# Laying out the tiles of triangular blocks and their transposed inverses with the block index innermost, in a fused recurrence and feed-forward kernel

## The chip, the cores and the metric

The kernel runs on one core of one Trainium2 chip. The metric is the device time of one execution in microseconds; three executions of the kernel before gave 995.05 us as their median (995.01 to 995.82). The engines are TensorE (PE in the rows, its weight loads PEld), VectorE (DVE), ScalarE (ACT), GpSimd (POOL) and SyncE (SP), which issues most of the DMAs. They run at the same time, each through its own list of instructions in a fixed order, and wait for one another by semaphores.

## What is computed

Four batches, 768 time steps and 320 channels (8 heads of 40) go through three parts, each of which takes the one before as its input:

```python
for t in range(S):                       # 1: a gated recurrence, per head a 40x40 state
    y[:, :, t] = einsum('bhd,bhde->bhe', r_t, state)
    Sa = einsum('bhde,bhe->bhd', state, a_t)
    state = state * w_t - einsum('bhd,bhe->bhde', Sa, b_t) + einsum('bhd,bhe->bhde', v_t, k_t)
h = maximum(x @ w_in, 0)                 # 2: feed-forward, 320 to 1024 to 320
x = (h * sigmoid(conv3(h))) @ w_out      #    gated by a convolution over time
u = x + real(fft(fft(x, axis=1), axis=2))            # 3: a Fourier mixing
out = u + maximum(layernorm(u) @ w_ch1, 0) @ w_ch2   #    and a second feed-forward
```

## The kernel before, in words

The change lies in part 1, in class `Attn`. The recurrence is worked in chunks of 64 time steps: 12 chunks, 4 batches and 8 heads. Within a chunk the update can be written as a triangular system of size 64 for each head and batch, so each (chunk, batch, head) has a unit triangular matrix whose inverse is needed. A 64x64 matrix is cut into two 32x32 triangular blocks on the diagonal and one full 32x32 block beside them.

Blocks are collected in groups. `group(c)` puts chunks 0 and 1 into groups 0 and 1 by themselves and then two chunks into each of groups 2 to 6, so there are seven groups. Tiles of a group are [128, 32, 32] or [128, 32, 64] in fp32: the 128 partitions hold the two blocks of two heads (two sets of rows of 64, each with a first and a second half of 32), and the free dimension holds a block index u (16 used in groups 0 and 1, 32 in the others; u counts chunk of the group, batch and pair of heads) and a column.

- `gram` (L189) makes the products of one chunk and batch on TensorE (L203). ScalarE copies the two triangular blocks with a minus sign into the tile `l0` (L218, L220) and the full block into `l1` (L219). In chunk 0 VectorE writes `l0` (L215) and applies the mask at once. Each such instruction writes 4 blocks: 32 partitions x 128 elements. In the trace l0 and l1 are both shown as `l`.
- `grp_start` (L244) makes `l0`; for groups 0 and 1 GpSimd clears its unused half (L248).
- `inverse` (L292) turns the group: VectorE transposes every 32x32 block of `l0` into the tile `A`, in which the block index is innermost (L297); a chain of multiplications and additions on VectorE solves all blocks together (L317 and L320 for groups 2 to 6, L259 and L262 for groups 0 and 1). Then VectorE transposes `A` back: once into `t1`, block after block (L327, or L270), and twice into the two column halves of `tt`, the tile with the transposed inverses (L330; for groups 0 and 1 `inverse16` fills it with L269 and, after two rounds of small matmuls L278, with two L288 of half the size). GpSimd clears a quarter of each half of `tt` (L333). In the trace t1 is shown as `t`.
- The merge (from L334): for each half `hf` of the blocks, 32 small matmuls on TensorE (L344, into PSUM tile `bp`), two copies by ScalarE back into `t1` (L348), 32 small matmuls that read `t1` and a column half of `tt` (L357, into `mp`), and two copies by ScalarE into `tt` (L361). Groups 0 and 1 have one half, the others two.
- `stage_u` (L381) then uses `tt` in each of the 48 steps (chunk, batch): for each of four pairs of heads a weight load of 64 columns of `tt` and a matmul with 80 columns (L388). An fp32 matmul is shown in the trace as two pairs of load and matmul, so a step has 8.

The steps go on one after the other: `step` (L470) lists the stages of a step: u (L388), s (L409, then VectorE L414 and L418 and GpSimd), y (L442, L445), ut (L397), h (L372, L375), g (L428, then VectorE L432 makes `gt`, which L445 of the next step reads) and o (L456, L460, then VectorE L463). `run` (L542) spreads the gram of a later chunk, the chain of the next inverse and a stream of weight preparation for parts 2 and 3 (`prep`, L684 to L741) between the stages. Both the order in which `run` issues and a planner that works with its own estimates of durations set the order of instructions on each engine before the program starts; on the chip it is fixed. Parts 2 and 3 (`Moe`) begin when the last step's output is stored.

Of the kernel before, what the change touches and what calls it, by code (L numbers as in the profile page):

```python
# [18 lines left out]
B, H, S, D = 4, 8, 768, 40  # L19
C = 64  # L20
NCH = S // C
NG = 3
HG = 3
P3 = HG * D
# [56 lines left out]
class Attn:  # L81
    def __init__(self, ctx, tc, ins, xd):
        self.tc, self.nc, self.xd = tc, tc.nc, xd
        self.i = ins
        nc = self.nc
# [25 lines left out]
        self.slots = {}  # L111
        for k, n, m, shape in (("x", 10, 4, [128, 2, NG * P3]), ("lk", 8, 4, [128, 2, 4, C]), ("tt", 2, 1, [128, 32, 64])):
            self.slots[k] = [mid[j >= m].tile(shape, F32, name=f"{k}{j}") for j in range(n)]
# [75 lines left out]
    def gram(self, c, b):  # L189
        nc = self.nc  # L190
# [6 lines left out]
        gidx, j = group(c)  # L197
# [8 lines left out]
        gv = gp.rearrange("p (q e t) -> p q e t", q=4, e=2)  # L206
        l0, l1 = g["l0"], g["l1"]
        for p in range(2):
# [35 lines left out]
    def grp_start(self, gidx):  # L244
        l0 = self.early.tile([128, 32, 32], F32, name="l0", tag="l0", bufs=1)
        l1 = self.early.tile([128, 32, 32], F32, name="l1", tag="l1", bufs=2)
        if gidx < 2:
            self.nc.gpsimd.memset(l0[:, 16:32], 0.0)  # L248
        self.grp[gidx] = dict(l0=l0, l1=l1)
# [15 lines left out]
    def inverse16(self, fl, t1, tt):  # L265
        nc = self.nc
        A = fl[:, 0:1024].rearrange("p (t s) -> p t s", s=32)
        at = tt[:, :, 32:64]
        nc.vector.transpose(at.rearrange("p u t -> p t u"), A)  # L269
        self.last = nc.vector.transpose(t1.rearrange("p u j -> p j u"), A.rearrange("p t j -> p j t"))  # L270
        yield
        m1 = self.early.tile([128, 16, 16], F32, name="m1", tag="tmp", bufs=2)
        for k in range(2):
            xp = self.pst("xd")
            for u in range(16):
                for q in range(4):
                    r = slice(32 * q, 32 * q + (32 if k else 16))
                    nc.tensor.matmul(xp[32 * q:32 * q + 32, 16 * u:16 * u + 16], at[r, u],  # L278
                                     m1[r, u] if k else t1[r, u, 0:16], start=True, stop=True)
# [7 lines left out]
        for i in (1, 0):  # L287
            nc.vector.transpose(tt[:, 0:16, 32 * i:32 * i + 32], t1[:, 0:16])  # L288
            yield


    def inverse(self, gidx):  # L292
# [3 lines left out]
        A = fl[:, 0:1024].rearrange("p (t s) -> p t s", s=32)  # L296
        self.first = nc.vector.transpose(A, g["l0"].rearrange("p u t -> p t u"))  # L297
        yield
# [14 lines left out]
        else:  # L313
# [15 lines left out]
            for i in (1, 0):  # L329
                nc.vector.transpose(tt[:, :, 32 * i:32 * i + 32].rearrange("p u t -> p t u"), A)  # L330
                yield
        for p in range(2):
            nc.gpsimd.memset(tt[64 * p + 32:64 * p + 64, :, 0:32], 0.0)  # L333
        yield "merge"  # L334
# [15 lines left out]
        for hf in range(nhf):  # L350
            xp = self.pst("mp")
            for u in range(16):
                for p in range(2):
                    r0 = slice(64 * p, 64 * p + 32)
                    r1 = slice(64 * p + 32, 64 * p + 64)
                    uu = hf * 16 + u
                    nc.tensor.matmul(xp[r0, 32 * u:32 * u + 32], bm[r1, uu], tt[r1, uu, 32:64],  # L357
                                     start=True, stop=True)
            for p in range(2):
                r0 = slice(64 * p, 64 * p + 32)  # L360
                nc.scalar.copy(tt[r0, hf * 16:hf * 16 + 16, 32:64],  # L361
                               xp[r0].rearrange("p (u t) -> p u t", t=32))
            yield
# [17 lines left out]
    def stage_u(self, c, b):  # L381
# [5 lines left out]
        for q in range(4):  # L387
            nc.tensor.matmul(hu[64:128, 80 * q:80 * q + 80], tt[:, (j * B + b) * 4 + q],  # L388
                             self.hbd[b][:, q].rearrange("p a b -> p (a b)"), start=True, stop=True)
# [973 lines left out]
```

## Time and profile before

| | |
|---|---|
| median of three executions | 995.05 us |
| the profiled execution: time | 997.03 us |
| its span, first to last instruction | 995.3 us |
| PE busy (weight loads apart) | 906.7 us, 91% |
| PEld busy | 818.7 us, 82% |
| DVE busy | 684.1 us, 69% |
| ACT busy | 520.7 us, 52% |
| POOL busy | 456.5 us, 46% |
[...]

Matmuls overlap in a pipeline, so "PE busy" is the time in which some matmul was under way and not a measure of its work. [...] A time of an instruction is its own duration; where a row of the timeline joins several (x4, x128), its time is from the first one's start to the last one's end. "[1.05 <-DVE gt L432]" means that the engine was idle for 1.05 us before the instruction, and that by the semaphores it was VectorE's L432 on `gt` that ended the wait. Part 1 takes the first 497 us, parts 2 and 3 the rest.

### The profile page before, as it was taken

To read this page: it belongs to the slowest core of one execution; us is meant where nothing else is said; L and a number is where in the kernel's file an instruction comes from. 1 tells how busy PE (TensorE), PEld (TensorE's weight loads), DVE (VectorE), ACT (ScalarE), POOL (GpSimd) and SP (SyncE) were. 2 spreads that over 40 slices of the span, in tenths; PEclk is the share of its full clock that TensorE was granted. 3 is DMA by queue.
4 is the path that set the end of the run, shared out by engine and by line. 5 is a ranking of instruction groups with operands and counts; after the bars stand their busy time and mean duration, and the time that the engine had idled before them with its cause. 6 is when DMAs were issued, how large, how long until landed. Compare 5 with 4: busy or idle time off the path is not lost. (4 is left out here: it accounts for less than half of the span.)

```text
span 995.3 us, 21859 instructions
## 1 busy us (share of the span) xinstructions
PE 906.7 (91%) x8178; PEld 818.7 (82%) x8178; DVE 684.1 (69%) x1322; ACT 520.7 (52%) x1448; POOL 456.5 (46%) x528
## 2 busy tenths in 40 slices
PE   5568698999989999999999699989999999999997
PEld 3557587888878888998888587777879999999997
DVE  8895997997996996881278697879684535424321
ACT  5668387676766577334376566567464431212211
POOL 6575375665665464343168566765562121101000
PEclk8667599997997999999999899998999999999999
DMA  9624346565555364339344643112105000000000
GB/s 224 178 77 128 90 126 178 154 161 147 150 138 152 98 169 114 87 98 255 81 126 134 187 141 114 54 50 70 41 1 172 20 1 21 20 20 21 20 14 31
DMA packets 102878, 101.15 MB, mean 102 GB/s; under 512 B 47160, under 2 KB 89003, under 8 KB 102763
## 3 DMA queue, kind: packets, MB, share of 16 engines
q1 hardware_dynamic: 100795, 94.73, 34.3%
q0 software_dynamic: 1968, 4.93, 1.6%
q8 instruction: 67, 1.10, 0.5%
q14 instruction: 48, 0.39, 0.2%
HBM read 74.81 MB, written 20.76 MB: 96 GB/s over the span
## 5 line engine op out<-in xcount | busy, mean ns | idle before, releaser
L831 DVE SCALAR_TENSOR_TENSOR c<-h,cw,c 128x384 f32<-128x384 f32 x128 | 113.3, 890 | 21.0 <-ACT c L829 17.4
L1085 DVE SCALAR_TENSOR_TENSOR gl<-hp,gh 128x384 fp32r<-128x384 f32 x80 | 44.4, 557 | 111.3 <-ACT gh L1084 111.2
L848 PE MATMUL acc<-w_out_f,z 128*128 128x320 f32 x384 | 118.0, 446 | 2.8 <-POOL z L837 1.1
L1084 ACT ACTIVATE gh<-hp 128x384 fp32r<-128x384 f32 x80 | 39.3, 492 | 149.8 <-PE hp L655 149.6
L848 PEld LDWEIGHTS acc<-w_out_f,z 128*128 128x128 f32 x384 | 73.5, 196 | 27.0 <-ACT x L853 1.8
L655 PE MATMUL hp<-xh,w_in_h 128*128 128x386 f32 x192 | 76.3, 397 | 14.3 <-ACT h L822 14.3
L655 PE MATMUL hp<-uh,w_ch_h 128*128 128x384 f32 x240 | 82.3, 343 | 0.0
L655 PE MATMUL hp<-ul,w_ch_h 128*128 128x384 f32 x240 | 81.0, 337 | 0.0
L1108 POOL DMA_INDIRECT out<-o,rows x12 | 11.7, 978 | 150.8 <-DVE o L1103 131.9
L317 DVE TENSOR_TENSOR tmp<-A 128x30 f32<-128x30 f32 (+9 forms) x150 | 77.1, 514 | 3.3
L320 DVE TENSOR_TENSOR A<-A,tmp 128x30 f32<-128x30 f32 (+9 forms) x150 | 76.8, 512 | 3.5
L203 PE MATMUL gram<-abd,kb 120*128 120x192 f32 (+1 forms) x288 | 64.6, 371 | 13.4 <-DMA w<-in_w 6.9
L419 POOL TENSOR_TENSOR st<-st,sm 120x360 f32<-120x360 f32 x40 | 48.3, 1208 | 56.9 <-DVE sm L418 53.0
L1098 PE MATMUL acc<-w_ch_h,gh 128*128 128x320 f32 x240 | 73.2, 312 | 0.0
L1098 PE MATMUL acc<-w_ch_l,gh 128*128 128x320 f32 x240 | 73.0, 309 | 0.0
L203 PEld LDWEIGHTS gram<-abd,kb 120*128 120x128 f32 x288 | 56.0, 227 | 17.3 <-POOL lk L223 9.7
L655 PE MATMUL hp<-xl,w_in_h 128*128 128x386 f32 x192 | 67.1, 349 | 0.0
L736 POOL TENSOR_TENSOR pm<-pm,py 128x160 int32<-128x160 int32 (+2 forms) x64 | 45.0, 703 | 44.0 <-DVE pm L734 17.1
L832 ACT ACTIVATE c<-c 128x384 f32<-128x384 f32 x64 | 33.4, 522 | 60.5 <-DVE c L831 60.3
L161 POOL TENSOR_TENSOR kb<-kb,vx 120x768 f32<-120x768 f32 x24 | 44.0, 1833 | 45.5 <-DMA kb<-in_kb 25.3
L445 PE MATMUL yp<-x,gt 128*64 128x40 f32 x768 | 54.8, 233 | 10.1 <-DVE gt L432 10.1
L445 PEld LDWEIGHTS yp<-x,gt 128*64 128x64 f32 x768 | 51.0, 143 | 13.2 <-DVE gt L432 11.9
(226 smaller groups left out, 2585.9 us busy)
## 6 DMA issues: line engine op xcount, KB each, us to landing
kb<-in_kb SPq DMA_DIRECT2D x24, 360.0 KB
vbd<-in_vbd SPq DMA_DIRECT2D x24, 320.0 KB
xd<-xo SPq DMA_DIRECT2D x56, 90.0 KB
w<-in_w SPq DMA_DIRECT2D x24, 185.6 KB
a<-in_a SPq DMA_DIRECT2D x24, 180.0 KB
z<-in_zv SPq DMA_DIRECT2D x24, 180.0 KB
zt<-in_vt SPq DMA_DIRECT2D x24, 180.0 KB
rbd<-in_r SPq DMA_DIRECT2D x72, 60.0 KB
```

Of the source, the lines that this page charges most:

```text
L161: self.markp = nc.gpsimd.tensor_tensor(kb, kb, vx[:, :, 2:66].unsqueeze(2).to_broadcast([P3, 6, 2, C]), op=ALU.mult)
L203: nc.tensor.matmul(gp[:, 192 * gi:192 * gi + 64 * nh], d["kb"][:, bl * NG + gi].rearrange("p a b -> p (a b)"), abd[:, 0:nh, bl * NG + gi], ...
L317: nc.vector.tensor_tensor(tmp, A[:, s + 1:32, s:s + 1].to_broadcast([128, n, s]), A[:, s:s + 1, 0:s].to_broadcast([128, n, s]), op=ALU.mult)
L320: nc.vector.tensor_tensor(A[:, s + 1:32, 0:s], A[:, s + 1:32, 0:s], tmp, op=ALU.add)
L419: nc.gpsimd.tensor_tensor(self.st[b], self.st[b], t, op=ALU.add)
L445: nc.tensor.matmul(yp[0:64, D * h:D * h + D], gt[:, h], d["x"][:, bl, D * h:D * h + D], start=(c == 0), stop=True, skip_group_check=True)
L655: nc.tensor.matmul(out, l, r, start=(j == 0), stop=(j == len(ops) - 1))
L736: nc.gpsimd.tensor_tensor(m, m, y, op=ALU.add)
L831: nc.vector.scalar_tensor_tensor(c, h[:, j:HS + j], cw[:, f, j:j + 1], c, op0=ALU.mult, op1=ALU.add)
L848: nc.tensor.matmul(self.acc[t][:, 0:DM], z[:, ts], w[:, f], start=(f == 0), stop=(f == NF1 - 1))
L1085: nc.vector.scalar_tensor_tensor(gl, hp[:, 0:HS], 0.0, gh.bitcast(F32), op0=ALU.max, op1=ALU.subtract)
L1098: nc.tensor.matmul(self.acc[t][:, 0:DM], l[:, ts], r, start=(f == 0 and j == 0), stop=(f == NF2 - 1 and j == 2))
```

## The change

The last two dimensions of `l0` and `tt` change places: `l0[partition, block, column]` becomes `l0[partition, column, block]`, `tt` likewise ([128, 32, 64] becomes [128, 64, 32]). `A`, `t1` and `l1` stay as they were. The same instructions read and write the same elements; the step from one element to the next changes:

- VectorE's L297 reads `l0`, and L330 and L269 write `tt`, in one contiguous run of 1024 where the step was 32 or 64 elements (L330, L269: 64; L297: 32). L288 (512 elements) wrote runs of 32 and now writes with a step of 32 elements.
- ScalarE's L218 and L220 and VectorE's L215 wrote `l0` in runs of 32 and now write with a step of 32 elements, so does ScalarE's L361 into `tt`.
- TensorE read contiguous columns of `tt` in L278 (weights, 32 columns), L357 (the moving operand, 32 columns) and L388 (weights, 64 columns), and now reads them with a step of 32 elements (128 bytes).
- GpSimd's L333 clears contiguous runs of 1024 in place of 32 runs of 32, and L248 clears 32 runs of 16 in place of one of 512.

```diff
@@ -109,7 +109,7 @@
         self.sm = [self.pre.tile([P3, NG, P3], F32, name=f"sm{j}") for j in range(2)]
 
         self.slots = {}
-        for k, n, m, shape in (("x", 10, 4, [128, 2, NG * P3]), ("lk", 8, 4, [128, 2, 4, C]), ("tt", 2, 1, [128, 32, 64])):
+        for k, n, m, shape in (("x", 10, 4, [128, 2, NG * P3]), ("lk", 8, 4, [128, 2, 4, C]), ("tt", 2, 1, [128, 64, 32])):
             self.slots[k] = [mid[j >= m].tile(shape, F32, name=f"{k}{j}") for j in range(n)]
         self.hf, self.late, self.markd = {}, None, None
         self.grp = {}
@@ -204,7 +204,7 @@
                              d["kb"][:, bl * NG + gi].rearrange("p a b -> p (a b)"),
                              abd[:, 0:nh, bl * NG + gi], start=True, stop=True)
         gv = gp.rearrange("p (q e t) -> p q e t", q=4, e=2)
-        l0, l1 = g["l0"], g["l1"]
+        l0, l1 = g["l0"].rearrange("p t u -> p u t"), g["l1"]
         for p in range(2):
             mul = nc.scalar.mul
             r0, r1 = slice(64 * p, 64 * p + 32), slice(64 * p + 32, 64 * p + 64)
@@ -245,7 +245,7 @@
         l0 = self.early.tile([128, 32, 32], F32, name="l0", tag="l0", bufs=1)
         l1 = self.early.tile([128, 32, 32], F32, name="l1", tag="l1", bufs=2)
         if gidx < 2:
-            self.nc.gpsimd.memset(l0[:, 16:32], 0.0)
+            self.nc.gpsimd.memset(l0[:, :, 16:32], 0.0)
         self.grp[gidx] = dict(l0=l0, l1=l1)
 
 
@@ -265,8 +265,8 @@
     def inverse16(self, fl, t1, tt):
         nc = self.nc
         A = fl[:, 0:1024].rearrange("p (t s) -> p t s", s=32)
-        at = tt[:, :, 32:64]
-        nc.vector.transpose(at.rearrange("p u t -> p t u"), A)
+        at = tt[:, 32:64]
+        nc.vector.transpose(at, A)
         self.last = nc.vector.transpose(t1.rearrange("p u j -> p j u"), A.rearrange("p t j -> p j t"))
         yield
         m1 = self.early.tile([128, 16, 16], F32, name="m1", tag="tmp", bufs=2)
@@ -275,7 +275,7 @@
             for u in range(16):
                 for q in range(4):
                     r = slice(32 * q, 32 * q + (32 if k else 16))
-                    nc.tensor.matmul(xp[32 * q:32 * q + 32, 16 * u:16 * u + 16], at[r, u],
+                    nc.tensor.matmul(xp[32 * q:32 * q + 32, 16 * u:16 * u + 16], at[r, :, u],
                                      m1[r, u] if k else t1[r, u, 0:16], start=True, stop=True)
             xv = xp[:, 0:256].rearrange("p (u s) -> p u s", s=16)
             if k == 0:
@@ -285,7 +285,7 @@
                                                op0=ALU.mult, op1=ALU.add)
             yield
         for i in (1, 0):
-            nc.vector.transpose(tt[:, 0:16, 32 * i:32 * i + 32], t1[:, 0:16])
+            nc.vector.transpose(tt[:, 32 * i:32 * i + 32, 0:16].rearrange("p t u -> p u t"), t1[:, 0:16])
             yield
 
 
@@ -294,7 +294,7 @@
         g = self.grp[gidx]
         fl = self.early.tile([128, 33 * 32], F32, name="A", tag="A", bufs=1)
         A = fl[:, 0:1024].rearrange("p (t s) -> p t s", s=32)
-        self.first = nc.vector.transpose(A, g["l0"].rearrange("p u t -> p t u"))
+        self.first = nc.vector.transpose(A, g["l0"])
         yield
 
         def new():
@@ -327,10 +327,10 @@
             nc.vector.transpose(t1.rearrange("p u j -> p j u"), A.rearrange("p t j -> p j t"))
             yield
             for i in (1, 0):
-                nc.vector.transpose(tt[:, :, 32 * i:32 * i + 32].rearrange("p u t -> p t u"), A)
+                nc.vector.transpose(tt[:, 32 * i:32 * i + 32], A)
                 yield
         for p in range(2):
-            nc.gpsimd.memset(tt[64 * p + 32:64 * p + 64, :, 0:32], 0.0)
+            nc.gpsimd.memset(tt[64 * p + 32:64 * p + 64, 0:32], 0.0)
         yield "merge"
         bm = t1
         nhf = 1 if gidx < 2 else 2
@@ -354,11 +354,11 @@
                     r0 = slice(64 * p, 64 * p + 32)
                     r1 = slice(64 * p + 32, 64 * p + 64)
                     uu = hf * 16 + u
-                    nc.tensor.matmul(xp[r0, 32 * u:32 * u + 32], bm[r1, uu], tt[r1, uu, 32:64],
+                    nc.tensor.matmul(xp[r0, 32 * u:32 * u + 32], bm[r1, uu], tt[r1, 32:64, uu],
                                      start=True, stop=True)
             for p in range(2):
                 r0 = slice(64 * p, 64 * p + 32)
-                nc.scalar.copy(tt[r0, hf * 16:hf * 16 + 16, 32:64],
+                nc.scalar.copy(tt[r0, 32:64, hf * 16:hf * 16 + 16].rearrange("p t u -> p u t"),
                                xp[r0].rearrange("p (u t) -> p u t", t=32))
             yield
 
@@ -385,7 +385,7 @@
         tt = self.grp[gidx]["tt"]
         hu = self.pst("u")
         for q in range(4):
-            nc.tensor.matmul(hu[64:128, 80 * q:80 * q + 80], tt[:, (j * B + b) * 4 + q],
+            nc.tensor.matmul(hu[64:128, 80 * q:80 * q + 80], tt[:, :, (j * B + b) * 4 + q],
                              self.hbd[b][:, q].rearrange("p a b -> p (a b)"), start=True, stop=True)
         self.mark = nc.scalar.mul(d["z"][64:128, bl, 0:DM], hu[64:128, 0:DM], -1.0)
 
```

## Rows read from the trace of the kernel before

**Rows 1.** Windows: us, busy us of PE, PEld, DVE, ACT, POOL (instructions), clock, DMA share, GB/s.
```profile
250.00:300.00 50.00, 46.34 (x423) 41.20 (x422) 48.94 (x101) 34.01 (x115) 31.07 (x36) 0.97 0.54 146
450.00:500.00 50.00, 49.44 (x518) 44.47 (x517) 11.38 (x29) 19.84 (x52) 12.50 (x17) 1.00 0.63 169
```
**Rows 2.** Timeline: start us, us, instruction. TensorE's last of part 1, first of part 2.
```profile
497.49 0.19 PE L522 MATMUL rp<-ro,rs 120*1 120x1 f32 x2
497.61 0.44 PE L655 MATMUL hp<-xh,w_in_h 128*128 128x386 f32 x1
```
**Rows 3.** Groups by form, VectorE: out<-in shapes xcount | busy us, mean ns | idle before.
```profile
L330 DVE STREAM_TRANSPOSE tt<-A 128x1024 f32<-128x1024 f32 x10 | 18.5, 1929 | 0.0
L297 DVE STREAM_TRANSPOSE A<-l 128x1024 f32<-128x1024 f32 x7 | 13.7, 1964 | 15.8 <-ACT l L220 15.8
...
L215 DVE SCALAR_TENSOR_TENSOR l<-gram,mlt 32x128 f32<-32x128 f32 x16 | 4.7, 291 | 0.4
...
L288 DVE STREAM_TRANSPOSE tt<-t 128x512 f32<-128x512 f32 x4 | 2.5, 672 | 0.0
```
**Rows 4.** Timeline: transposes and merge of group 4, partly at the lower clock.
```profile
307.63 3.71 DVE L330 STREAM_TRANSPOSE tt<-A 128x1024 f32<-128x1024 f32 x2
...
311.43 0.67 DVE L432 TENSOR_TENSOR gt<-gp,mlt 128x512 f32<-128x512 f32 x1
...
312.24 1.44 PE L428 MATMUL gp<-rbd,zt 120*128 120x192 f32 x6 [1.23 <-ACT t L348]
...
313.61 3.62 PE L357 MATMUL mp<-tt,t 32*32 32x32 f32 x128
...
315.57 1.16 ACT L361 COPY tt<-mp 32x512 f32<-32x512 f32 x2 [2.83 <-PE mp L357]
317.16 1.06 PE L388 MATMUL u<-hbd,tt 128*64 128x80 f32 x6
```
**Rows 5.** Timeline: the same in group 3.
```profile
234.12 1.82 PE L428 MATMUL gp<-rbd,zt 120*128 120x192 f32 x6 [1.05 <-DVE gt L432]
...
238.75 1.16 ACT L361 COPY tt<-mp 32x512 f32<-32x512 f32 x2
...
240.01 1.30 PE L388 MATMUL u<-hbd,tt 128*64 128x80 f32 x8
```
**Rows 6.** Timeline: a transpose of group 1 and what stood behind it.
```profile
74.57 1.90 DVE L269 STREAM_TRANSPOSE tt<-A 128x1024 f32<-128x1024 f32 x1
...
78.75 0.55 PE L409 MATMUL sp<-z,x 128*120 128x120 f32 x1 [3.40 <-DVE st L414]
```
**Rows 7.** Waits: who waited for whom, us in total, times, longest us.
```profile
DVE A L297 <- ACT l L220: 15.8, 4, 6.2
...
ACT t L348 <- DVE tt L288: 10.7, 1, 10.7
```
**Rows 8.** Timeline: the first stage u, of group 0.
```profile
60.84 1.33 PE L388 MATMUL u<-hbd,tt 128*64 128x80 f32 x8 [2.31 <-POOL tt L333]
```
**Rows 9.** By line and tile: ns min/median/max, first and last start us, form.
```profile
L220 ACT ACTIVATE l<-gram x88: 270/272/275, 28.9 to 395.3; 32x128 f32<-32x128 f32 x88
...
L278 PEld LDWEIGHTS xd<-t,tt x256: 101/115/154, 40.2 to 99.6; 16*32 16x32 f32 x128
...
L361 ACT COPY tt<-mp x24: 570/576/577, 58.6 to 449.3; 32x512 f32<-32x512 f32 x24
```
**Rows 10.** Timeline: a stage u at full clock, its eight loads and eight matmuls.
```profile
429.87 0.61 PEld L388 LDWEIGHTS u<-hbd,tt 128*64 128x64 f32 x8
429.87 0.77 PE L388 MATMUL u<-hbd,tt 128*64 128x80 f32 x8
```
**Rows 11.** Timeline: end of the merge of group 5, at full clock.
```profile
389.41 2.21 PE L357 MATMUL mp<-tt,t 32*32 32x32 f32 x128
...
390.66 2.35 ACT L361 COPY tt<-mp 32x512 f32<-32x512 f32 x4 [1.42 <-PE mp L357]
...
391.87 0.49 PE L388 MATMUL u<-hbd,tt 128*64 128x80 f32 x4 [0.25 <-ACT tt L361]
```

## The prediction, made before the change was timed

> **What bounds the kernel now.** I read the windows first, then the groups of VectorE by form, then the timeline around the places where the changed tiles are made and used. In 250 to 300 us VectorE is busy for 48.94 of 50 us and PE for 46.34; in 450 to 500 us PE is busy for 49.44 and VectorE for 11.38 [rows 1]. So part 1 is held by VectorE in some steps and by TensorE in others, and in the merges, where a group's inverses are finished, by a chain that runs through PE and ScalarE. TensorE's last matmul of part 1 starts at 497.49, the first of part 2 at 497.61 [rows 2]: parts 2 and 3 follow at once, and no changed instruction stands in them. A microsecond won or lost at the end of part 1 is counted as one at the end of the kernel.
>
> **VectorE's transposes.** The change takes the long step out of 19 transposes of 1024 elements: ten L330, seven L297 and two L269. They take 1.93 to 1.96 us each [rows 3]. No transpose of before with two contiguous sides has 1024 elements; L288, which has runs of 32 on one side, takes 0.672 us for 512 [rows 3]. Twice that is 1.34, the upper bound for 1024 contiguous elements. From L215's 128 elements in 0.291 to L288's 512 in 0.672 the slope is 0.99 ns an element and some 0.16 us are fixed; 512 more at this slope give 1.18, the lower bound. I take 1.2, as the two L288 halves of the first bound count the fixed part twice: 0.73 saved each (0.6 to 0.78), 13.9 us of VectorE's time in all. The four L288 now write with a step, as L330 does: between half of 1.93 and half of 1.93 + 0.16, 0.97 to 1.05, so 0.35 more each. L327 and L270 stay as they were.
>
> What of it lies on the path:
> 1. Group 4's two L330 end at 311.34, and L432 (`gt`), which they held up, runs 311.43 to 312.10; TensorE's L428 then starts at 312.24 after 1.23 us of idleness [rows 4]. The row names ScalarE's L348, but VectorE's end lies 0.14 us before the start. With the transposes 1.46 shorter the gap goes: 1.2 us. In group 3 the same L428 waits 1.05 us for `gt` by the row's own words [rows 5]: 1.05. In group 2 VectorE is full too, but the next wait is on ScalarE: half, 0.7. In groups 5 and 6 TensorE has other work: 0.
> 2. In group 1, TensorE's L409 is idle for 3.40 us until VectorE's L414, which stands behind L269 (and L270) in its queue [rows 6]: 0.72.
> 3. L297 starts a group's chain, and in four groups VectorE sat idle before it, 15.8 us in all, for ScalarE's L220 [rows 7]. For groups 3 to 5, whose chains end in steps that VectorE fills, I count half of 3 x 0.76: 1.1. Group 6 runs in PE's stretch: 0.
> 4. Group 0 starts the kernel: L297 and L269 win 1.48, eight L215 directly ahead of L297 write with a step and lose (128 elements x 0.71 ns, the price worked out below) 0.73. The first stage u waits for GpSimd's L333 in the end [rows 8], so of the 0.75 left I count half: 0.4.
>
> That is 5.2 us of the 13.9; the rest is covered by TensorE and by waits. Against it, group 1's L348 waits for both L288 [rows 7]: 0.7 lost.
>
> **ScalarE's writes.** L361 (512 elements, 0.576 us) and L218 and L220 (128 elements, 0.272, 176 of them) now write with a step of 128 bytes [rows 9]. No ScalarE instruction of before does that. Lower bound: nothing. Upper: what the step costs VectorE, 0.73 us / 1024 = 0.71 ns an element. VectorE's is the only stepped fp32 write in the trace, so I take it: L361 becomes 0.94, L218 and L220 0.36.
>
> **TensorE's reads.** Stage u loads 64 columns of `tt` eight times in 0.61 us and goes through in 0.77 [rows 10]: 76 ns a load, 96 ns a pair. L357 streams 32 columns 128 times in 2.21 us [rows 11], 17 ns each, two of them side by side on different rows: 35 ns for one. No load or matmul of before reads with a step. Lower bound: nothing, if the array takes a column too slowly to notice. Upper: again 0.71 ns a column, 45 ns on a load and 23 on an L357. I take the upper end, since the only stepped accesses that the trace shows all pay, whether they read (L297) or write (L330). Then a load takes 121 ns, more than the 96 of its pair, and stage u grows by 8 x 25 = 0.2 us. L357 grows from 17 to 29 ns, 0.75 us for a half group. At the lower clock it already takes 3.62 us for 128, 28 ns each [rows 4], and stage u 1.30 [rows 5], 163 ns a pair: there the step hides, and I count 0. L278's weights are 512 loads of 32 columns in groups 0 and 1 (256 shown [rows 9]), four side by side: at most 512 x 23 / 4 ns = 2.9 us. I count 0, since PE is not the late engine in that stretch (VectorE and GpSimd are [rows 6, 8]), and keep 2.9 for the range.
>
> [...]
>
> **What that does on the path.** In the merge, stage u starts right behind the first half's two L361: in group 3 copies from 238.75 to 239.91, u at 240.01 [rows 5]; in group 5 copies from 390.66, two of four done at 391.82, u at 391.87 [rows 11]. Groups 1, 2 and 6 look the same. Two copies more dear by 0.36 each delay u by 0.73 in groups 1, 2 and 3; in group 4 there are 0.4 us of slack (316.73 to 317.16 [rows 4]), so 0.4; in groups 5 and 6, where the clock is full, L357's first half adds 0.75 to it, 1.5 each. Group 0 is covered by GpSimd [rows 8]. Sum 5.5 us.
>
> Stage u at full clock: 16 steps in PE's stretch at the end and about 10 more between, where PE is busy from one u to the next. 26 x 0.2 = 5.2 us; the other 22 are hidden behind VectorE or the lower clock.
>
> The four L218 and L220 of a chunk and batch take 0.36 us more. ScalarE has room (34.0 of 50 us [rows 1]), except where L297 waits for the last of them [rows 7]: half of 3 x 0.36, 0.5. GpSimd's L333 and L248 clear as many elements as before: 0, and GpSimd is not ahead of anyone but in group 0.
>
> **The sum.** Won 5.2; lost 0.7 + 5.5 + 5.2 + 0.5 = 11.9; 6.7 us slower. The profiled execution took 997.03 us (span 995.3), so 1003.7 for it; the median of the runs is 995.05, and set on it I predict 1001.7.
>
> **Rivals.**
> - *The step is free for ScalarE and TensorE.* Then only VectorE's terms stand: 5.2 won, 0.7 lost, 4.5 faster, 990.5. [...] The point from which it decides: if L388's loads and L361 stay at 76 ns and 0.576 us. [...] Chance 0.26.
> - *Only ScalarE pays.* L361 costs 0.73 in groups 1, 2, 3, 5 and 6 and 0.4 in group 4, 4.0; with 0.5 and 0.7 it balances the 5.2: 995.1. Chance 0.17.
> - *The costs land everywhere.* Stage u pays in all 48 steps (4.4 more) and the second halves' copies, which stand before `z` on ScalarE, delay it by 0.73 in five groups (3.6): 1009.7. The same would come if u had now to wait for both halves, whose columns lie in between each other: 1.16 us of copies in five groups, 5.8 more. Chance 0.08.
> - *The transposes don't get faster*, because 32x32 blocks and not steps set their time: 5.2 lost from the sum, 1006.9. L288's 1.31 ns an element against L330's 1.88 speaks against it. Chance 0.03.
>
> **How the numbers follow.** My forecast, every price at VectorE's, has 0.46, with a range of its own of 997 to 1007: 26 steps could be 16 or 36 (2 us each way) and the halves that I counted none or whole (3). As cases of both signs hold much of the chance, the range reaches down to the free case and up to most of the dear one: 989 to 1009, which leaves out about a tenth at each end. A measurement tells about 0.2%, 2 us, from nothing. Faster: nearly all of the first rival, a fifth of the second and a little of the forecast, 0.30. Same: most of the second, a twelfth of the others, 0.17. Slower: 0.53.
>
> **What would show it.** Right, step by step: L330, L269 and L297 at 1.15 to 1.34 us, L288 near 1.0; L361 near 0.94 and L218 and L220 near 0.36; the eight loads of a stage u at full clock near 0.97 us and an L357 half near 1.85. L428's wait for `gt` in groups 3 and 4 gone, the start of u in groups 5 and 6 about 1.5 us further behind the start of L357, and TensorE's first matmul of part 2 at about 504. Wrong: if L388 and L361 keep their durations the forecast falls and the first rival stands; if the planner, which sees other tiles, puts instructions in another order, terms 1 and 3 may come out otherwise.

## The result, and the profile after

The changed kernel takes 1013.5 us (median of six runs, 1011.3 to 1018.0) against 996.8 for the kernel before: a ratio of 1.0148, with a 95% interval of 1.0116 to 1.0181. A second set of runs gave 1.0160 (1.0121 to 1.0200). That is 15 us slower, where 6.7 were forecast. The profiled execution took 1011.6 us with a span of 1009.9; before it was 997.03 and 995.3.

Both kernels issue the same instructions; only the steps between elements of the changed operands differ. VectorE, ScalarE and GpSimd show them in the same order in both traces, and TensorE too, but for some places where matmuls of stage u start among those of a neighbouring stage. First the windows of the changed kernel, with the columns of [rows 1], and the end of part 1, as [rows 2] shows it of before:

```profile
250.00:300.00 50.00, 47.65 (x424) 42.73 (x422) 48.96 (x100) 36.00 (x115) 32.20 (x35) 0.97 0.52 144
450.00:500.00 50.00, 49.65 (x537) 45.21 (x530) 8.62 (x22) 20.00 (x46) 13.26 (x20) 0.83 0.53 154
```
```profile
513.77 0.19 PE L522 MATMUL rp<-ro,rs 120*1 120x1 f32 x2
513.89 0.45 PE L655 MATMUL hp<-xh,w_in_h 128*128 128x386 f32 x1
```

Part 2 starts 16.3 us later (513.89 against 497.61), so the whole loss, and 1.7 us more, lies in part 1. In the late window TensorE is as busy as before, but its granted clock is 0.83 instead of 1.00.

The changed groups by form (columns as in [rows 3]; ScalarE's before are in [rows 9]):

```profile
L361 ACT COPY tt<-mp 32x512 f32<-32x512 f32 x24 | 24.4, 1017 | 9.9 <-PE mp L357 9.6
...
L330 DVE STREAM_TRANSPOSE tt<-A 128x1024 f32<-128x1024 f32 x10 | 11.7, 1217 | 0.0
L297 DVE STREAM_TRANSPOSE A<-l 128x1024 f32<-128x1024 f32 x7 | 8.7, 1237 | 21.1 <-ACT l L220 21.1
L215 DVE SCALAR_TENSOR_TENSOR l<-gram,mlt 32x128 f32<-32x128 f32 x16 | 6.1, 382 | 0.4
L288 DVE STREAM_TRANSPOSE tt<-t 128x512 f32<-128x512 f32 x4 | 3.8, 1018 | 0.0
```

VectorE's transposes are as fast as was hoped, 1.22 and 1.24 us where they took 1.93 and 1.96, and ScalarE's L361 is 0.44 us dearer. Note how L297's idle time grew from 15.8 to 21.1 us: part of what VectorE saved came back as waiting. Stage u in the last steps, first its weight loads, then the matmuls (timeline; [rows 10] before):

```profile
428.15 0.96 PEld L388 LDWEIGHTS u<-hbd,tt 128*64 128x64 f32 x8
```
```profile
428.16 1.11 PE L388 MATMUL u<-hbd,tt 128*64 128x80 f32 x8
```

It takes 1.11 us where it took 0.77. (Steps are counted here by stage u, 0 to 47, from one to the next; the first steps of groups 2 to 6 are 8, 16, 24, 32 and 40.) The timeline of group 4's merge ([rows 4] before) and group 5's ([rows 11]):

```profile
308.20 2.32 DVE L330 STREAM_TRANSPOSE tt<-A 128x1024 f32<-128x1024 f32 x2
...
310.65 0.67 DVE L432 TENSOR_TENSOR gt<-gp,mlt 128x512 f32<-128x512 f32 x1
...
311.89 1.08 PE L428 MATMUL gp<-rbd,zt 120*128 120x192 f32 x6
...
389.69 3.80 PE L357 MATMUL mp<-tt,t 32*32 32x32 f32 x128
...
391.71 4.08 ACT L361 COPY tt<-mp 32x512 f32<-32x512 f32 x4 [2.21 <-PE mp L357]
...
393.79 1.26 PE L388 MATMUL u<-hbd,tt 128*64 128x80 f32 x8 [0.30 <-ACT tt L361]
```

In group 4 the idle time of 1.23 us before L428 is gone, as forecast. In group 5, L357 takes 3.80 us instead of 2.21, though the clock is full (1.00 in both), and stage u starts 4.10 us behind its start instead of 2.46. Last, the step that follows each of the merges of groups 2 to 6, from one stage u to the next (windows, columns as in [rows 1]: the last three are granted clock, DMA share and GB/s):

```profile
162.40:170.25 7.85, 7.85 (x64) 6.98 (x64) 3.17 (x9) 7.27 (x19) 1.47 (x3) 0.80 0.51 147
240.85:248.89 8.04, 8.04 (x68) 7.36 (x68) 2.91 (x8) 7.22 (x19) 2.35 (x5) 0.80 0.54 142
317.06:325.60 8.54, 8.54 (x62) 7.63 (x63) 3.12 (x9) 6.36 (x17) 1.00 (x2) 0.68 0.45 123
393.79:401.74 7.95, 7.95 (x64) 7.09 (x65) 2.45 (x6) 6.56 (x17) 0.73 (x1) 0.79 0.01 2
456.08:463.69 7.61, 7.61 (x53) 6.80 (x53) 0.00 (x0) 3.92 (x8) 0.00 (x0) 0.50 0.92 275
```

The same five steps of the kernel before:

```profile
161.72:169.71 7.99, 7.99 (x64) 7.05 (x64) 4.11 (x10) 6.22 (x19) 1.58 (x3) 0.79 0.59 175
240.01:248.69 8.68, 8.68 (x69) 7.85 (x68) 4.00 (x9) 6.33 (x19) 3.40 (x5) 0.74 0.56 149
317.16:325.94 8.78, 8.78 (x67) 7.87 (x63) 3.69 (x8) 5.46 (x17) 1.32 (x2) 0.66 0.42 120
391.87:398.53 6.66, 6.38 (x64) 5.65 (x65) 2.74 (x5) 5.52 (x17) 0.73 (x1) 1.00 0.17 44
448.80:453.05 4.25, 4.25 (x54) 3.82 (x54) 0.00 (x0) 2.68 (x8) 0.00 (x0) 1.00 0.87 240
```

Before, the clock was low behind the merges of groups 2 to 4 and full behind the last two; here it falls behind all five. Together the five steps are only 3.6 us longer than before (39.99 against 36.36). Most of the loss shows in the last 16 steps, from stage u of step 32 to part 2: the kernel before, the changed kernel, its step 41 alone (the second step behind group 6's merge; 6.31 us before), and the last 16 steps in a second profile of it, which comes further below:

```profile
391.87:497.61 105.74, 104.61 (x1305) 94.44 (x1306) 55.45 (x123) 42.70 (x115) 29.98 (x41) 1.00 0.47 125
393.79:513.89 120.10, 119.19 (x1305) 108.26 (x1305) 53.60 (x123) 46.02 (x116) 29.96 (x41) 0.91 0.39 109
463.69:474.06 10.37, 10.37 (x66) 9.46 (x65) 1.43 (x4) 2.02 (x7) 1.87 (x5) 0.56 0.87 282
397.68:512.52 114.84, 113.93 (x1306) 103.75 (x1306) 53.59 (x123) 45.57 (x115) 29.98 (x41) 0.97 0.41 113
```

The stretch is 14.4 and 9.1 us longer than before; up to its start 1.9 and 5.8 us were lost.

### The profile page after: what moved, and what is told of

Its sections match the earlier page's. It is cut to its first block, busy times and chain, and to the rows that moved or that the text cites. A ratio compares the mean times of both kernels' runs of the same rounds, so it can differ in the third digit from the quotient of the medians.

```text
span 1009.9 us, 21859 instructions
## 1 busy us (share of the span) xinstructions
PE 926.2 (92%) x8178; PEld 838.3 (83%) x8178; DVE 677.0 (67%) x1322; ACT 545.3 (54%) x1448; POOL 455.9 (45%) x528
## 5 line engine op out<-in xcount | busy, mean ns | idle before, releaser
L831 DVE SCALAR_TENSOR_TENSOR c<-h,cw,c 128x384 f32<-128x384 f32 x128 | 110.3, 866 | 19.3 <-ACT c L829 15.7
L848 PE MATMUL acc<-w_out_f,z 128*128 128x320 f32 x384 | 114.2, 435 | 3.4 <-POOL z L837 1.2
L848 PEld LDWEIGHTS acc<-w_out_f,z 128*128 128x128 f32 x384 | 71.2, 190 | 26.4 <-POOL z L835 2.0
L655 PE MATMUL hp<-xh,w_in_h 128*128 128x386 f32 x192 | 76.1, 396 | 14.5 <-ACT h L822 14.4
L203 PE MATMUL gram<-abd,kb 120*128 120x192 f32 (+1 forms) x288 | 64.0, 369 | 11.9 <-DMA w<-in_w 7.0
L203 PEld LDWEIGHTS gram<-abd,kb 120*128 120x128 f32 x288 | 55.3, 224 | 15.8 <-POOL lk L223 7.2
L388 PE MATMUL u<-hbd,tt 128*64 128x80 f32 x384 | 55.2, 293 | 8.0 <-issue 4.1
```

What stands on the lines that cost most here:

```text
L203: nc.tensor.matmul(gp[:, 192 * gi:192 * gi + 64 * nh], d["kb"][:, bl * NG + gi].rearrange("p a b -> p (a b)"), abd[:, 0:nh, bl * NG + gi], ...
L388: nc.tensor.matmul(hu[64:128, 80 * q:80 * q + 80], tt[:, :, (j * B + b) * 4 + q], self.hbd[b][:, q].rearrange("p a b -> p (a b)"), start=T ...
L655: nc.tensor.matmul(out, l, r, start=(j == 0), stop=(j == len(ops) - 1))
L831: nc.vector.scalar_tensor_tensor(c, h[:, j:HS + j], cw[:, f, j:j + 1], c, op0=ALU.mult, op1=ALU.add)
L848: nc.tensor.matmul(self.acc[t][:, 0:DM], z[:, ts], w[:, f], start=(f == 0), stop=(f == NF1 - 1))
```

## The experiments

Times against the kernel before are (ratio - 1) x 997 us. One theory, A, was that TensorE's stepped reads of `tt` carry the loss; its rivals were ScalarE's writes (B) and a clock that fell by chance (C).

**Which tile?** `l0` alone (the diff's lines for `l0` put on the kernel before), and `tt` alone (the rest):

> Before, with l0 alone in the new layout (blocks innermost): L297 reads contiguous rows, ScalarE's L218 and L220 write elements 128 bytes apart; tt as before. Theory A (the loss is TensorE's stepped reads of tt, with the granted clock that falls behind them): no loss here, 0 to -1 us against the kernel before (L297 saves 0.73 us in the groups where the step waits for it; L218 and L220 cost 0.115 us each, hidden). Theory B (ScalarE's stepped writes hold up the steps, in the gram stage too): slower by 3 us or more, since 64 grams at 0.27 us more of ScalarE stand in the step. Theory C (the low clock from 455 to 473 us is chance): as A.

> The changed kernel with l0 back in the layout of before, tt alone in the new one. Theory A: the whole loss, +13 to +16 us against before, with the low granted clock behind the merge of group 6 again. Theory B: +8 to +11 us, the gram stage's part gone. Theory C: +7 us (loss without the low clock), or +14 with it, at random.

`l0` alone: 0.9989 (0.9964 to 1.0013), no difference that can be told. `tt` alone: 1.0115 (1.0077 to 1.0154), most of the loss: 11.5 us, below A's 13 to 16 and just above B's 8 to 11, with an interval that reaches into both. L218 and L220 at 0.385 us and L297 at 1.24 either show in nothing or cancel. B's part about the gram stage falls.

**One cost taken out of the change at a time.** Stage u's loads, in groups 2 to 6:

```
- tt[:, :, k]
+ tt.rearrange("p t u -> p (t u)")[:, s0:s0 + 64]     s0 = 961 + k for k < 16, else 64 * k
```

> The changed kernel, with stage u's weight loads (L388) of groups 2 to 6 reading 64 contiguous columns of tt, chosen so that they wait for the same half of the merge; the weights are the wrong columns, so this part of the computation is changed. Theory A: load and matmul fall from 205 and 275 ns back to about 137 and 233, stage u at full clock from 1.11 to 0.77 us, and steps 33 to 38 and 42 to 45 from 6.66 to 6.31 us; some 25 steps are paced by it: +5 to +8 us against before instead of +15, and less where the low clock goes too. Theory B: +12 us or more; the steps keep 6.66 us because ScalarE is what paces them.

1.0029 (1.0002 to 1.0056), 2.9 us: 12 us less than the changed kernel. The timeline gives back what the steps lost: steps 34 to 38 take 6.31 us each, as before, instead of 6.66, and the clock stays full behind the last two merges (1.00 in both steps). Stage u in one of them:

```profile
435.60 0.77 PE L388 MATMUL u<-hbd,tt 128*64 128x80 f32 x8
```

The second product of the merge, and ScalarE's copy:

```
- bm[r1, uu], tt[r1, 32:64, uu]
+ bm[r1, uu], tt[r1, 32 + 2 * u:34 + 2 * u, hf * 16:hf * 16 + 16]
```
```
- scalar.copy(tt[r0, 32:64, hf * 16:hf * 16 + 16].rearrange("p t u -> p u t"), ...)
+ scalar.copy(tt[r0, 32:64, hf * 16:hf * 16 + 16], ...)
```

> The changed kernel, with the second product of the merge (L357) reading its 32 columns as two runs of 16 contiguous elements of tt instead of 32 elements 128 bytes apart; the columns are the wrong ones, so this part of the computation is changed. Theory A: 128 products at full clock fall from 3.80 to 2.2 us; if the low clock behind the merge of group 6 comes from this slow product, full clock is granted from 455 to 473 us, and the kernel is at +4 to +7 us against before (1.6 us a merge in two or three merges, 6.8 us of clock). Theory B: the product falls too, but the wait moves to L361 and the low clock stays: +11 to +13 us. Theory C: +11 us, the low clock anywhere.

> The changed kernel, with ScalarE's copy at the end of the merge (L361) writing runs of 16 contiguous elements into tt instead of elements 128 bytes apart; the products land at the wrong places of their block, so this part of the computation is changed. Theory A (stage u's stepped loads carry most of the loss, the merge's two lines the rest, and the clock falls with the loads, not with the copy): L361 falls from 1.02 to about 0.58 us, the merge of groups 5 and 6 from 4.1 to 3.6 us between L357's start and stage u; 0.45 us in each of some four merges, so 1 to 3 us less than the changed kernel: +11 to +14 us against before, low clock at 456 us still there. Theory B (ScalarE's stepped writes): +5 us or less, low clock gone.

Without L357's step: 1.0082 (1.0053 to 1.0110). Without L361's: 1.0124 (1.0104 to 1.0143). L357 falls to 2.21 us, L361 to 0.58, but in both profiles the clock is still low behind all five merges: so neither of these two is needed for that. The first (8.2 us, the low clock still there) lies between A's 4 to 7 and the 11 to 13 of the others; the second (12.4 us) is A's case. With both of TensorE's reads mended:

> The changed kernel with both of TensorE's reads of tt made of contiguous runs (stage u's loads in groups 2 to 6 and L357, edits as in the two runs with one of them), L361 and l0's writes as in the change; these parts of the computation are changed. If the two costs add (11.9 us for the loads, 6.6 us for L357 by those runs): -2 to -6 us against before, faster than before although ScalarE's writes are still stepped. If they share one cause, the low clock, so that taking either away gives most of it: 0 to +3 us.

1.0005 (0.9978 to 1.0033): 0.5 us, between -2.2 and +3.3. Taken out one at a time, the two are worth 12.5 and 7.2 us of the changed kernel's 15.4 (the mean of both sets); if they added, -4.3 would be left. So they overlap by about 5 us, with an uncertainty as large (the four half-intervals added in squares). The 0.5 us lie in the range of the second expectation, and the interval reaches into the first. But the low clock is not simply the cause that the two share: in this profile, with both reads mended, it still falls behind group 5's merge (0.55 in a step of 11.41 us).

**Is stage u dear by itself?** The kernel before, with its loads alone stepped (64 columns 64 bytes apart in its own `tt`):

```
- tt[:, (j * B + b) * 4 + q]
+ tt.rearrange("p u t -> p (u t)")[:, s0:s0 + 1009:16]     s0 = 1024 * (k // 16) + k % 16
```

> The kernel before, with stage u's weight loads (L388) alone reading 64 columns that lie 64 bytes apart in its own tt; the columns are the wrong ones of the same half, so this part of the computation is changed. Theory A1 (the stepped loads cost 0.34 us in each step that TensorE paces, and they alone bring the low granted clock behind the merges of groups 5 and 6): stage u 1.11 us at full clock, +9 to +13 us against before, with low stretches near 392 and 449 us. Theory A2 (the loads cost 0.34 us a step; the low clock needs the slow merge as well): +6 to +9 us, full clock from 344 us to the end of the part. Theory B (ScalarE): within 2 us of before.

1.0049 (1.0024 to 1.0075): 4.9 us, below what both variants named. Stage u is 1.11 us as in the change; the last merge keeps full clock behind it, as A2 had it, but group 5's does not (0.81 in the step), as A1 had it. The same change of loads is worth 5 us here and 12 there.

**The same kernel again,** to see whether the low clock is its own:

> The changed kernel once more, without an edit. If the low granted clock behind the merges of groups 5 and 6 belongs to this kernel: low stretches near 394 and 456 us in this profile too, the second 3 to 17 us long, and a ratio of 1.011 to 1.018. If it was chance: none of them, or elsewhere.

It is there behind all five merges again, in the last for 3.4 us instead of 17. So that the clock falls behind the last two merges as well belongs to this kernel; for how long does not.

**What does a step cost?** A probe behind the kernel's own work:

> The kernel before, with a stretch of its own behind the work: 16 weight loads of 64 columns and 40 moving columns, at steps of 1, 2, 4, 8, 16 and 32 elements between columns; 16 products with 128 moving columns at the same steps; ScalarE's and VectorE's copies of 512 elements out of PSUM at steps of 1, 2, 4, 8 and 32 elements, and in runs of 2 with a hop of 32. Theory A (a price for each column that lies apart from the one before): loads at step 32 cost 139 ns a pair where step 1 costs about 96, L361's kind 2.0 ns against 1.1 an element; and the price is reached by degrees or at one step, which the rows tell (at 2 elements still that of step 1, if pairs are free; at 32 the full one). Theory B (the price comes from the tile's other users, not from the step): all steps alike, within 5%.

Groups by form of the probe. L1128, L1130, L1132 and L1138 load 64 columns at steps of 1, 2, 4 and 32 elements; L1142 and L1144 stream 128 columns at 2 and 4; L1152 to L1160 are ScalarE's copies at 1, 2, 4 and 32 (L1158, at 8, left out), L1172 its copy in runs of two; L1162 to L1166 VectorE's at 1, 2 and 4:

```profile
L1144 PE MATMUL pb<-probe,one 128*64 128x128 f32 x32 | 7.4, 404 | 0.0
...
L1156 ACT COPY probe<-pc 128x512 f32<-128x512 f32 x4 | 4.2, 1055 | 0.1
L1166 DVE COPY probe<-pc 128x512 f32<-128x512 f32 x4 | 4.2, 1054 | 0.1
L1160 ACT COPY probe<-pc 128x512 f32<-128x512 f32 x4 | 4.0, 1012 | 0.1
...
L1132 PE MATMUL pa<-one,probe 128*64 128x40 f32 x32 | 4.0, 291 | 0.0
...
L1142 PE MATMUL pb<-probe,one 128*64 128x128 f32 x32 | 3.8, 275 | 0.0
...
L1138 PE MATMUL pa<-one,probe 128*64 128x40 f32 x32 | 3.7, 310 | 0.0
...
L1164 DVE COPY probe<-pc 128x512 f32<-128x512 f32 x4 | 2.8, 692 | 0.1
L1162 DVE COPY probe<-pc 128x512 f32<-128x512 f32 x4 | 2.8, 691 | 112.4 <-ACT probe L1160 112.3
L1154 ACT COPY probe<-pc 128x512 f32<-128x512 f32 x4 | 2.4, 607 | 0.1
L1172 ACT COPY probe<-pc 128x512 f32<-128x512 f32 x4 | 2.3, 587 | 19.0 <-DVE probe L1170 18.9
L1152 ACT COPY probe<-pc 128x512 f32<-128x512 f32 x4 | 2.3, 585 | 98.0 <-PE pb L1150 97.9
L1130 PE MATMUL pa<-one,probe 128*64 128x40 f32 x32 | 2.1, 231 | 0.0
L1128 PE MATMUL pa<-one,probe 128*64 128x40 f32 x32 | 2.1, 230 | 0.0
```

Read busy time, since groups of one kind have the same count. Two elements apart (8 bytes) is free or nearly so on all three engines: 2.1 and 2.1 us, 585 and 607 ns, 691 and 692. Four apart (16 bytes) costs nearly twice on TensorE and ScalarE (4.0 us, 1055 ns) and half as much again on VectorE (1054 ns), and 32 apart costs no more than four (3.7 us, 1012 ns). The price comes at once, between 8 and 16 bytes. (From the loads at 8 to those at 32 the granted clock was 0.58, from the loads at 1 to those at 4 1.00. The streaming row at one element, between that stretch and one at 1.00, has 5.8 us where two elements have 3.8, and is left out.) Worked out for one element or column, the price is 0.93 ns for TensorE ((4.0 - 2.1) us over 32 x 64 columns), 0.92 for ScalarE and 0.71 for VectorE (470 and 363 ns over 512).

These rows show the price for TensorE and ScalarE as well, which the rows of before could not.

**A layout without the price.** If two elements apart are free, then so should be a tile with blocks in adjacent pairs, `[128, 16, 64, 2]`: VectorE writes runs of two (in the probe its copy in runs of two, L1174, took 692 ns, L1162 691), TensorE and ScalarE step by 8 bytes. All uses of `tt` are changed alike:

```
- ("tt", 2, 1, [128, 64, 32])
+ ("tt", 2, 1, [128, 16, 64, 2])
- nc.vector.transpose(tt[:, 32 * i:32 * i + 32], A)
+ nc.vector.transpose(tt[:, :, 32 * i:32 * i + 32].rearrange("p a t b -> p t a b"),
+                     A.rearrange("p t (a b) -> p t a b", b=2))
- tt[:, :, (j * B + b) * 4 + q]
+ tt[:, (j * B + b) * 2 + q // 2, :, q % 2]
...
```

> The changed kernel with tt laid out in adjacent pairs of blocks, [128, 16, 64, 2]: VectorE's transposes write runs of two elements, TensorE and ScalarE step by 8 bytes instead of 128; l0 as in the change. [...] If pairs keep VectorE's gain and a step of 8 bytes costs TensorE and ScalarE nothing: L330 stays at 1.22 us, L388 goes back to 137 and 233 ns, L357 to 17 ns each, L361 to 0.58 us: -3 to -6 us against before, and -18 us or more against the changed kernel. If every step between columns costs the same, whatever its size: L388 stays at 205 and 275 ns, +10 to +15 us. If pairs do not help VectorE: L330 1.9 us and the kernel where the kernel before is, 0 to -1 us.

> As the kernel with tt in adjacent pairs of blocks, but with l0 in the layout of before. If l0's new layout brings nothing that the step sees (run with l0 alone: ratio 0.9989, 0.9964 to 1.0013), this one is within 2 us of the other; if ScalarE's L218 and L220 (0.115 us more each) cost the step, this one is the faster by 1 to 4 us; if L297's 0.73 us in groups 2 to 6 is on the path, the slower by 1 to 3 us.

> The kernel in pairs once more, without an edit, on the chip of the three runs with one cost each: a ratio of 0.992 to 0.997 against before, and the base that those three are read from.

0.9948 (0.9922 to 0.9974) and, again, 0.9945 (0.9926 to 0.9964); with `l0` as before 0.9941 (0.9922 to 0.9960). All three are faster than the kernel before by 5 to 6 us, and than the changed kernel by some 20. Groups by form of the first:

```profile
L388 PE MATMUL u<-hbd,tt 128*64 128x80 f32 x384 | 38.2, 244 | 9.3 <-POOL tt L333 3.1 <-issue 2.8 <-ACT lk L222 1.3
...
L388 PEld LDWEIGHTS u<-hbd,tt 128*64 128x64 f32 x384 | 30.4, 142 | 13.7 <-issue 3.6 <-POOL tt L333 3.2 <-ACT lk L222 1.5
...
L361 ACT COPY tt<-mp 32x512 f32<-32x512 f32 x24 | 14.6, 608 | 7.1 <-PE mp L357 6.8
...
L330 DVE STREAM_TRANSPOSE tt<-A 128x1024 f32<-128x1024 f32 x10 | 11.7, 1218 | 0.0
```

L330 keeps the whole gain (1218 ns, 1217 in the change), L361 loses 0.03 us (608 ns against 576), and stage u's loads and matmuls are back at 142 and 244 ns, where the kernel before has 144 and 248.

**One cost at a time onto that kernel,** the other way round:

```
pairs + u:     tt.rearrange("p a t b -> p (a t b)")[:, s0:s0 + 1009:16]
pairs + L357:  tt[r1, hf * 8:hf * 8 + 8, 32 + u // 2:64:8, u % 2]
pairs + L361:  tt[r0, hf * 8:hf * 8 + 8, 32:64].rearrange("p a t b -> p (t b) a")
```

> The kernel with tt in pairs and l0 as in the change (every stepped cost gone, VectorE's gain kept: 0.9948, -5.2 us), with stage u's loads alone stepped again (64 columns 64 bytes apart, the wrong columns of the same half: this part of the computation is changed). Theory A3 (each cost alone is near the prediction's term, and the rest of the loss comes only where slow loads and a slow merge meet): 4 to 7 us above the kernel in pairs, so 0 to +2 us against before; steps 33 to 38 at 6.66 us, full clock behind the merge of group 6. Theory A4 (the loads alone carry 12 us, as their removal from the changed kernel said): +6 to +8 us against before.

> The same kernel in pairs, with the merge's second product (L357) alone reading elements at least 64 bytes apart (the wrong columns, so this part of the computation is changed). A3: 128 products 3.8 us instead of 2.2 at full clock, half of it ahead of the first L361: 0.8 us on each of five or six merges at most, so 2 to 5 us above the kernel in pairs, -3 to 0 us against before. A4: 0 to 2 us above it.

> The same kernel in pairs, with ScalarE's copy at the end of the merge (L361) alone writing elements 512 bytes apart (they land at the wrong places of their block, so this part of the computation is changed). A3: 1.02 us instead of 0.61, twice in a row ahead of stage u: 0.8 us on each of seven merges, so 4 to 6 us above the kernel in pairs, -1 to +1 us against before. A4: 2 to 3 us above it, as its removal from the changed kernel said.

With u: 0.9987 (0.9965 to 1.0009). With L357: 0.9999 (0.9977 to 1.0021). With L361: 1.0015 (0.9993 to 1.0036). From the pairs' -5.3 us that is 4, 5 and 7 us. A4, by which the loads alone carry 12, falls; A3 holds for the loads, and its sizes for L357 and L361 were a little low.

All of it in one table. "Low" is the time at the lower clock in the five steps behind merges, from their windows (per row: length x (1 - clock) x 2, since the clock records in the traces of before and after hold only 1.00 and 0.50), in one profiled execution; "last 16" is the stretch from stage u of step 32 to part 2, in the same execution:

```
stepped                      against before, us   five steps, us   low, us      steps low   last 16, us
kernel before                      0              36.4             13.9         3           105.7
  with the new l0                 -1.1            32.4              6.5         1           105.3
  with u                          +4.9            36.4             10.8         3           112.8
nothing (pairs)                 -5.2, -5.5        30.3, 34.8        0, 8.9      0, 2        106.3, 106.7
  with l0 as before               -5.9            34.7              8.8         2           106.6
u                                 -1.3            32.5              3.4         1           110.3
L361                              +1.5            34.6              9.8         2           106.9
L361 (both reads in runs)         +0.5            38.6             18.1         3           111.8
L357                              -0.1            40.0             22.8         5           113.8
L357 and L361                     +2.9            37.4             16.2         3           107.4
u and L361                        +8.2            40.8             21.7         5           116.1
u and L357                       +12.4            39.2             19.0         5           114.2
u, L357 and L361               +14.8, +16.0       40.0, 38.3       22.8, 17.6   5, 5        120.1, 114.8
  with l0 as before              +11.5            39.5             21.6         5           115.8
```

In the two rows where the changed kernel's stage u reads runs (L357 and L361; L361, both reads in runs), groups 0 and 1 are still stepped. The last four columns need a caution, since they come from single executions, not all of them typical. The one with L357 alone was the longest of its twelve (1004.1 us, their median 995.5), so its low clock is not that of most; the first in pairs was the fastest of its ten (984.3, median 990.4), and the one with u and L357 the fastest of its six (1002.9, median 1008.8).

Stage u costs 4 us without a slow merge (-5.35 to -1.3) and 12.5 with one (+2.9 to +15.4). The difference, 8.4 us, has an uncertainty of some 4.6 (the four half-intervals added in squares): a joint part that is more than chance. Its size depends on the way of counting. Added to the pairs one at a time, the three costs are 4.0, 5.3 and 6.9 us, 16.2 of the 20.8 us that lie between the pairs and the changed kernel, because L357 and L361 cost more one by one (12.1) than together (8.2). That leaves 4.6 us for the meeting, with an uncertainty of 5.6. The windows show where the clock is low. The five steps of the kernel in pairs:

```profile
158.92:165.31 6.39, 6.39 (x65) 5.60 (x65) 3.23 (x9) 6.17 (x18) 1.53 (x3) 1.00 0.54 160
234.40:240.95 6.55, 6.55 (x68) 5.95 (x69) 3.32 (x9) 6.36 (x19) 3.21 (x4) 1.00 0.44 119
306.51:312.50 5.99, 5.99 (x62) 5.31 (x62) 2.19 (x5) 5.49 (x17) 1.80 (x3) 1.00 0.55 153
379.48:386.57 7.09, 6.39 (x64) 5.66 (x64) 2.36 (x6) 5.83 (x17) 0.73 (x1) 1.00 0.13 35
436.93:441.18 4.25, 4.25 (x53) 3.82 (x54) 0.00 (x0) 2.73 (x8) 0.00 (x0) 1.00 0.96 302
```

and with u stepped:

```profile
159.43:166.16 6.73, 6.73 (x65) 5.95 (x65) 3.40 (x10) 6.47 (x19) 1.47 (x2) 1.00 0.55 146
235.60:244.04 8.44, 8.44 (x68) 7.64 (x69) 3.29 (x9) 6.67 (x19) 3.19 (x4) 0.80 0.56 154
310.61:316.94 6.33, 6.33 (x63) 5.66 (x63) 2.19 (x5) 5.55 (x17) 1.63 (x3) 1.00 0.49 135
...
```

The steps 8, 16 and 24 take 6.0 to 6.7 us in these two profiles at full clock, and 7.7 to 9.1 where a part of the step runs at the lower one, in the second profile in pairs, with u, and in the changed kernel. The changed kernel's five steps exceed the first profile in pairs by 9.7 us, of which stage u's own 0.34 explains 1.7; but they exceed the second by only 5.2, and the kernel before by 3.6. So the first three of these steps vary from one execution to the next, whatever the kernel.

The last 16 steps are steadier. With none of the three costs (the first two rows of the table and the three in pairs) the clock is full in all of them, in five profiles of five. With stage u and at least one line of the merge stepped, it falls behind both merges in five profiles of five. With one cost, or the merge's two, it falls behind both in one of six (L357 alone), behind group 5's alone in two, and behind neither in three. So slow loads and a slow merge together make the low clock there likelier, but either of them alone can be followed by it too; what trips it is not settled. Nor is the split between low clock and longer merges more than an estimate from single executions.

## Why the prediction was wrong

The direction was right, and so were nearly all prices; the size was wrong by more than the range allowed.

- **VectorE's gain: right.** L330, L269 and L297 came to 1.22, 1.23 and 1.24 us (1.2 forecast), L288 to 1.02 (near 1.0). 5.2 us of 13.9 were to reach the end, and the kernels in pairs, which have the gain and none of the price, win 5.2 to 5.9. Its places were mixed, so the sum fits better than its parts: L409's wait in group 1 fell from 3.40 to 0.83 us, but L409 started only 0.80 us earlier (77.95), near the 0.72 counted, and `l0`'s terms (1.1 and part of 0.4) show no effect that can be told.
- **ScalarE's price: right.** L361 1.02 us (0.94 forecast), L218 and L220 0.385 (0.36).
- **Stage u: the product held by luck, through two errors.** The eight loads came to 0.96 us (0.97 forecast). But I counted of a load only what exceeds the 96 ns of a pair of load and product, 0.2 us a stage; the stage grew by 0.34 us, the whole growth of its loads. Against it, 26 steps were to pay, and by the time of the kernel in pairs some 12 do (4 us / 0.34); ten of them can be seen in the second profile, steps 33 to 38 and 41 to 44, each longer by 0.34 us or a little more (6.66 instead of 6.31, step 33 6.45 instead of 6.10). So 5.2 us were forecast, and 4 to 5 are paid when u is the only cost.
- **The merges: the delay was right, its cost was not.** L357 takes 29.7 ns (29 forecast). From its start to stage u, groups 0 to 6 lost 0, 1.0, 0.7, 0.2, 0.6, 1.6 and 1.6 us, 5.7 in all (5.5 forecast). But with u unstepped the two lines cost 8.2 us (-5.3 to +2.9), and with u stepped 16.7 (-1.3 to +15.4).
- **The step that failed** is "What that does on the path": it adds 5.5 us for the merges and 5.2 for stage u as if each stood alone and the clock stayed as before, full from 344 us on. Up to stage u of step 32 the forecast has 2.0 us lost, and the two profiles have 1.9 and 5.8. For the last 16 steps it has 4.7 (16 x 0.2 for stage u, 1.5 for group 6's merge), and 14.4 and 9.1 were lost. Step 39, with group 6's merge, took 14.61 us instead of 12.62. Behind the merges of groups 5 and 6 the clock fell, where it had been full: steps 32, 40 and 41 took 25.9 and 20.7 us together, instead of 17.2. By the times, the merge's two lines cost 8.2 us without stage u's slow loads and 16.7 with them, so that some 8 us, give or take 4.6, came on top where the two met. Losses of 11.9 us were forecast, and 20 are there (15 and the gain of 5). Whether the low clock is all of what came on top, and what trips it, stays open.
- **The rivals.** The free step is refuted by L388 and L361, the case that only ScalarE pays by L388, and slow transposes by L330. "The costs land everywhere" (0.08) came nearest, with 1009.7, but for another reason: no stage u pays at the lower clock (1.30 to 1.33 us at 0.50 in both kernels), and the first of group 5 still starts behind two of the four copies (at 393.79, while the four run from 391.71 to 395.79).

## What to carry to other kernels

A step of 16 bytes between fp32 elements cost TensorE, ScalarE and VectorE about the same in the probe, 0.7 to 0.9 ns an element, and steps of 32 to 128 bytes about as much, so taking it from one engine's operand hands the bill to whoever else uses the tile. Before choosing between two layouts, look for the one in between: pairs of elements kept VectorE's 37% (1.93 to 1.22 us), cost TensorE nothing and ScalarE 0.03 us a copy. And where a chain of small products between long steps gets longer, do not take the clock of the profile before for granted in the steps behind it; their price belongs in the range.

## What the runs showed of the hardware

- In the probe the price of a step is all or nothing: 8 bytes free, 16 bytes full, 128 bytes no more than 16 (2.1, 4.0 and 3.7 us for the loads, the last in the stretch at 0.58 of the clock).
- What is stepped gains nothing from the full clock in L357: in the changed kernel a merge's 128 stepped records take 3.80 us at a clock of 1.00 (group 5) and 3.81 at 0.87 (group 4), about what contiguous ones took, 3.62 us, at 0.50 [rows 4], and 62 of group 0's, all at 0.50, take 2.00 us where contiguous ones took 1.91. And stage u pays nothing for the step at the lower clock: it takes 1.30 us at 0.50 in both kernels [rows 5].
- ScalarE's L219, contiguous itself but issued between the stepped L218 and L220, went from 0.253 to 0.298 us, with `l0` alone in the new layout too; with `l0` as before it is at 0.253. The runs do not tell why.
